# One more half chunk projected by seven block products, and three weight sums moved from the Vector engine to GpSimd

## The chip, the cores and the metric

The kernel runs on one core of a Trainium2 chip. The engines of that core have short names in the profile: PE (TensorE, matrix products; PEld is its weight load), DVE (VectorE), ACT (ScalarE), POOL (GpSimd) and SP (SyncE, whose queue issues all DMAs of this kernel). The metric is the device time of one execution in microseconds (us), the median over several runs.

## The reference

A DeltaNet layer is followed by a two-layer MLP without gating.

```python
# q, k, v: (4, 8, 768, 48); beta: (4, 8, 768)
k_n = k / (norm(k) + 1e-6)
for t in range(768):
    y[:, :, t] = q[:, :, t] @ state
    v_old = state^T k_n[:, :, t]
    state += beta[:, :, t] * outer(k_n[:, :, t], v[:, :, t] - v_old)
# y -> x of shape (3072, 384); w_in (384, 2048), w_out (2048, 384), both float64
h = x @ w_in
g = h / (1 + exp(-h))
out = g @ w_out          # (3072, 384) float32
```

## The kernel before

The sequence of 768 tokens is cut into six chunks of 128. In each chunk the four batches with eight heads each are worked on together. A chunk goes through these steps: `prepare` (transposes of keys and queries, and the score blocks of each head), `invert` (a unit triangular matrix in each 32 by 32 block is inverted), `solve` (the inverses are merged to larger blocks, the new values are found and the states updated) and `feed_forward` (the MLP on the 512 tokens of the chunk, in two halves `hf` of two batches each).

`feed_forward(c)` is a generator. Each `next` issues one piece of the MLP, and the program deals these pieces out by hand between the steps of the next chunk's attention. Within each engine the order of instructions is fixed: `pin` ties every instruction to the one issued before it on its engine, and `in_line` does the same for the DMAs of SP. So the order of the calls is the order in which each engine works, and an engine whose next instruction waits does nothing else.

A half of the MLP has two parts. `hidden(c, hf)` makes eight tiles `phid` in PSUM, each from 12 profile records on PE (a matrix product of 32-bit numbers shows as two records); ACT turns each by Silu into `gT` (L729). The tiles rotate through a pool `psM` of two PSUM buffers, so PE can be at most two tiles ahead of ACT. The second part is the product with `w_out`. There are two ways to do it:

- `project(c, b, o)`, used for both halves of chunk 0: for each of two batches, 16 products with 384 columns each, eight pieces of two products.
- `combine(c, hf)`, used in all later chunks: the two batches are the two rows of a 2 by 2 block matrix, `gT`'s even and odd feature blocks are its columns, and `w_out` is a 2 by 2 block matrix as well. Seven products of blocks (Winograd's form of Strassen's method) take the place of eight. It has seven chains of eight products with 192 columns, 14 pieces of four products each. It needs sums of blocks of `g`, made by DVE in `sum_g` (named S1 to S4), and sums of blocks of `w_out`, made once by `sum_w`.

`sum_w` has eight steps of 128x768 elements each: six write the three tiles `sums_of_w`, and the last two overwrite one block of `w_out` in place. The in-place steps destroy values that `project` still needs, so they have to stand behind the last `project`. All eight are DVE instructions (L776), the six behind `invert(1)` and the two within `prepare(2)`.

`invert(c)` is a chain of rank-one updates on DVE, 30 pairs of a product (L477) and an addition (L481), each waiting for the one before it, both with two inputs in SBUF. At its end ACT copies one half of the result (L485) and DVE the other (L486), SP writes both to DRAM and reads them back in the layout that `solve` wants (L492, L502). The generator yields 32 times.

GpSimd, before `invert(1)` starts, does the integer additions of `narrow` (L181), which makes 32-bit weights from the 64-bit ones. Its last instruction before `solve(1)` is the last of these.

The part of the program that the change touches begins after `prepare(1)`: 22 of chunk 0's 64 pieces have been issued when the loop over `invert(1)` starts, that is all of `hidden(0, 0)` and six pieces of `project`. The loop and the lines behind it deal out 28 more before `solve(1)`, which takes 12, and the last two follow it.

Of the kernel before, what the change touches and what calls it, by code (L numbers as in the profile page):

```python
# [21 lines left out]
def kernel(  # L22
# [22 lines left out]
    nc = tc.nc  # L45
# [15 lines left out]
    FG = 3  # L61
# [12 lines left out]
    def bank(pool, tag, name):  # L74
        return pool.tile([P, 512], FP32, name=name, tag=tag)
# [3 lines left out]
    def behind(later, earlier, how=NoSync):  # L79

        tc.add_manual_dep(
            later.ins, earlier.ins.name,
            mybir.DependencyInfo(how, mybir.DependencyReason.DATA), reason="order",
        )
# [3 lines left out]
    def pin(op):  # L88

        engine = op.ins.engine  # L90
        if engine in pins:
            behind(op, pins[engine])
        pins[engine] = op
        return op
# [35 lines left out]
    def load_v(i):  # L130
        if i < N and i not in vfs:
            vfs[i] = load.tile([P, H, D], FP32, name="vf", bufs=4)
            in_line(nc.sync.dma_start(out=vfs[i][:], in_=chunk_of(v, i)))
# [123 lines left out]
    for t in bkbufs:  # L257
# [4 lines left out]
        out=above[:], in_=above[:], pattern=[[1, P]], compare_op=ALU.is_gt, fill=0.0,  # L262
# [33 lines left out]
    def squares(c):  # L296

        sums[c] = small.tile([P, BH], FP32, name="ss", bufs=1)[:]
        for b in range(B):
            if c == 1:  # L300
                sq = packed(zbufs[b])
            else:
                if b % HB == 0:
                    two = work.tile([P, HB, H, D], FP32, name="sq", tag="xg"[b // HB], bufs=1)
                sq = two[:, b % HB]
            pin(nc.scalar.activation(
                out=sq, in_=packed(kbufs[(c * B + b) % NK]), func=ACTF.Square
            ))
            pin(nc.vector.tensor_reduce(
                out=sums[c][:, b * H : (b + 1) * H], in_=sq, axis=AX.X, op=ALU.add  # L310
            ))
# [401 lines left out]
    def hidden(c, hf):  # L713

        for f in range(NFF // 2):
            ph = bank(psM, "m", "phid")
            for j in range(2):
                for a in range(NKT):
                    pin(nc.tensor.matmul(  # L719
                        ph[:, j * GT : (j + 1) * GT],  # L720
                        lhsT=w_in[:, a, (2 * f + j) * P : (2 * f + j + 1) * P],
                        rhs=xTs[c, hf][:, a, :],
                        start=(a == 0), stop=(a == NKT - 1),
                    ))
                if j == 0:
                    yield
            if f % FG == 0:
                gTs[f // FG] = mlp.tile([P, FG, 2 * GT], FP32, name="gT", bufs=3)
            pin(nc.scalar.activation(  # L729
                out=gTs[f // FG][:, f % FG, :], in_=ph[:], func=ACTF.Silu, scale=0.5  # L730
            ))
            if c > 0 and f % FG == 1 and f >= FG:
                for which in (S1, S2):
                    sum_g(which, f // FG - 1)
            yield

    def project(c, b, o):

        po = bank(psM, "m", "po")
        for f in range(NFF):  # L740
            at = (f % 2) * GT + (b % HB) * C
            pin(nc.tensor.matmul(  # L742
                po[:, 0:DM], lhsT=gTs[f // 2 // FG][:, f // 2 % FG, at : at + C],
                rhs=w_outs[f // HFF][:, f % HFF, :], start=(f == 0), stop=(f == NFF - 1),
            ))
            if f == NFF - 1:
                pin(nc.scalar.mul(o[:, b % HB], po[:, 0:DM], 0.5))
                row = b * S + c * C
                in_line(nc.sync.dma_start(out=out[row : row + C, :], in_=o[:, b % HB]))
            if f % 2 == 1:  # L750
                yield
# [6 lines left out]
    def quarters(i, j, m):  # L758
        t = w_outs[i][:].rearrange("p (a j) (n m) -> p a j n m", j=2, n=2)
        return t[:, :, j, m]  # L760

    def sum_w():


        n = HFF // 2
        for k, left, right, op in (
            (0, (1, 1), (0, 1), ALU.subtract), (1, 0, (0, 0), ALU.add), (2, (1, 0), 1, ALU.subtract),
            (None, (0, 1), (0, 0), ALU.subtract),
        ):
            for i in range(2):  # L770
                of = [
                    quarters(i, *x) if isinstance(x, tuple) else sums_of_w[x][:, n * i : n * (i + 1)]
                    for x in (left, right)
                ]
                to = of[0] if k is None else sums_of_w[k][:, n * i : n * (i + 1)]
                yield pin(nc.vector.tensor_tensor(out=to, in0=of[0], in1=of[1], op=op))  # L776


    S1, S2, S3, S4 = (
# [7 lines left out]
    def sum_g(which, g):  # L787
        k, left, right, op = which
        fs = group(g)
        of = [  # L790
            sums_of_g[:, x, fs] if isinstance(x, int) else
            gTs[g][:, 0 : fs.stop - fs.start, x[0] * GT + x[1] * C : x[0] * GT + (x[1] + 1) * C]
            for x in (left, right)
        ]
        pin(nc.vector.tensor_tensor(out=sums_of_g[:, k, fs], in0=of[0], in1=of[1], op=op))  # L795
# [64 lines left out]
    def feed_forward(c):  # L860
        for hf in range(2):
            yield from hidden(c, hf)
            if c > 0:
                yield from combine(c, hf)
                continue
            o = mlp.tile([P, HB, DM], FP32, name="o", bufs=1)
            for b in range(hf * HB, (hf + 1) * HB):
                yield from project(c, b, o)
# [4 lines left out]
    def go(steps, n=1):  # L873
        for _ in range(n):
            next(steps, None)

    def prepare(c, us):

        for b in range(B):
            i = c * B + b  # L880
            if len(us) == b:
                us.append(list(turn(i, A, CC))[0])
                yield
            for _ in score(i, us[b], (A, CC)):
                pass
            block_out(i, us[b])
            block_in(i)
            scale(i)
            load_k(i + B)
            size(i)  # L890
            yield
# [81 lines left out]
    def until(piece):  # L973
        while piece is not None and piece not in narrowed:
            fill(1)
# [8 lines left out]
    for b in range(B):  # L984
        size(b)
    more(1, ("in", 1))
    pieces = feed_forward(0)
    for n, _ in enumerate(solve(0, us)):
        fill(2)
# [19 lines left out]
    inv = invert(1)  # L1009
# [1 line left out]
        until(("out", min(7, n + 2)))  # L1011
        go(pieces)
    until(("out", 7))
    for n in range(20):
        go(inv, 2)
        go(pieces)
    us = next_us
    go(inv, 99)
    sums_made = sum_w()
    for n in range(8):  # L1020
        go(pieces)
        if n < 6:
            go(sums_made)
    for n, _ in enumerate(solve(1, us)):
        go(pieces, 2 if n in (1, 2) else 1)
        if n == 5:
# [3 lines left out]
    for n in range(2 * B, 3 * B):  # L1030
        load_v(n)
    go(pieces, 999)
    pieces = feed_forward(1)

    for c in range(1, NCH):
        if c + 1 < NCH:
            us = []
            for n, _ in enumerate(prepare(c + 1, us)):
                go(pieces)
                if n in (2, 4):  # L1040
                    go(sums_made)
            go(pieces, 4)
            inv = invert(c + 1)
            n = 0
            for _ in inv:
                n += 1
                if n % 5 in (0, 1, 3, 4):
                    go(pieces)
            go(pieces, 7)
            for n, _ in enumerate(solve(c + 1, us)):  # L1050
                go(pieces, 2 if n in (1, 2) else 1)
                if n == 5 and c + 2 < NCH:
                    squares(c + 2)
                if n == 6 and c + 2 < NCH:
                    norms(c + 2)
            for n in range((c + 2) * B, (c + 3) * B):
                load_v(n)
        go(pieces, 999)
        if c + 1 < NCH:
            pieces = feed_forward(c + 1)  # L1060
# [30 lines left out]
```

## Time and profile before

| | us |
|---|---|
| median of 3 runs | 770.54 (770.52 to 770.78) |
| the profiled execution's own time | 770.21 |
| its span in the profile | 768.5 |
| PE busy | 730.4 (95% of the span) |
| PEld busy | 630.0 |
| DVE busy | 411.8 |
| ACT busy | 233.3 |
| POOL busy | 83.6 |
| PE work in 250 us to 768 us | without a gap in the 40-slice view, but for the last slice |
| PE idle between 140 and 171 us | 1.11, 1.80 and 1.64 |

Start times are counted from the start of the span. Engine columns of a view of windows give busy time and, in brackets, the number of instructions. In a timeline a row begins with its start and its duration, both in us, and what stands in square brackets at its end is how long the engine sat idle before it and what ended the wait. The ends of matrix products are modelled, so a busy PE isn't PE at its peak; that is why pitches (the distance of starts in a run of equal products) are used for sums over PE.

### The profile page before, as it was taken

The page shows a single profiled execution, that of the slowest core. Times are in us where ns is not written, and L with a number is a line of the kernel's source. Part 1 is how long each engine was busy: PE and PEld are TensorE (multiplying, and loading weights), DVE is VectorE, ACT ScalarE, POOL GpSimd, SP SyncE. Part 2 cuts the span into 40 slices and gives each one's busy share as a digit, 9 for nine tenths or more (in the row PEclk, how much of TensorE's full clock was granted, in tenths as well). Part 3 has the DMA queues.
Part 4 walks back from the last instruction along what each step waited for, and adds up shares of the span by engine and source line. Part 5 has one row for each costly group of instructions (what it writes and reads, how often), then busy time and mean ns, then how long its engine had stood idle before and what let it go on. Part 6 is the DMA issues. An engine that isn't in the chain of part 4 may idle for free.

```text
span 768.5 us, 16585 instructions
## 1 busy us (share of the span) xinstructions
PE 730.4 (95%) x6806; PEld 630.0 (82%) x6806; DVE 411.8 (54%) x1050; ACT 233.3 (30%) x512; POOL 83.6 (11%) x95
## 2 busy tenths in 40 slices
PE   7549799899999999999999999999999999999997
PEld 5336587478777999997999997999998999999987
DVE  4886678892336672445672445672445682221212
ACT  4524465311325212315212315212315212312020
POOL 4005246300003000002000002000002000000000
PEclk8859999999999999999999999999999999999999
DMA  9798847212025213034113044113043013010000
GB/s 164 116 167 162 172 146 194 52 66 42 13 54 106 42 48 70 6 77 101 33 49 69 5 77 96 38 49 70 5 77 77 15 49 70 5 30 0 21 1 21
DMA packets 155067, 50.93 MB, mean 66 GB/s; under 512 B 142544, under 2 KB 147536, under 8 KB 154992
## 3 DMA queue, kind: packets, MB, share of 16 engines
q1 hardware_dynamic: 154992, 49.87, 31.1%
q8 instruction: 54, 0.88, 0.5%
q14 instruction: 21, 0.17, 0.1%
HBM read 34.70 MB, written 14.16 MB: 64 GB/s over the span
## 4 chain that ended last, share of the span: by engine, by line
PE 88%; DVE 4%; DMA 3%; SPq 2%; issue 1%; ACT 1%; POOL 1%; ACTq 0%; DVEq 0%
PE phid L719 31%; PE px L813 14%; PE py L813 11%; PE pa L399 6%; PE pz L583 4%; PE pt L376 3%; PE po L742 3%; PE pw L276 3%; PE pyc L642 3%; PE pyc L614 2%; PE ph L567 2%; DMA z<-in_q_dram 2%; PE px L551 2%; PE py L551 2%; PE pu L625 2%; DVE x L481 1%
## 5 line engine op out<-in xcount | busy, mean ns | idle before, releaser
L719 PE MATMUL phid<-xT,w_in 128*128 128x256 f32 x1152 | 260.7, 382 | 2.2 <-ACT gT L729 1.6
L719 PEld LDWEIGHTS phid<-xT,w_in 128*128 128x128 f32 x1152 | 214.8, 190 | 37.2 <-issue 6.3
L729 ACT ACTIVATE gT<-phid 128x512 f32<-128x512 f32 x96 | 57.3, 598 | 189.6 <-PE phid L719 149.2
L415 DVE SCALAR_TENSOR_TENSOR ap<-pa,g,above 128x128 f32<-128x128 f32 x192 | 58.2, 376 | 43.7 <-ACT ap L409 43.7
L481 DVE TENSOR_TENSOR x<-x,rank 128x30 f32<-128x30 f32 (+9 forms) x180 | 59.6, 331 | 7.4 <-ACT x L470 1.1
L477 DVE TENSOR_TENSOR rank<-g,x 128x30 f32<-128x30 f32 (+9 forms) x180 | 59.4, 330 | 5.0
L795 DVE TENSOR_TENSOR sums_of_g<-gT 128x384 f32<-128x384 f32 (+1 forms) x60 | 29.2, 509 | 57.9 <-ACT gT L729 47.3
L813 PE MATMUL py<-w_out,sums_of_g 128*128 128x192 f32 x320 | 56.8, 329 | 0.0
L813 PE MATMUL px<-sums_of_w,sums_of_g 128*128 128x192 f32 x320 | 56.8, 329 | 0.0
L813 PEld LDWEIGHTS px<-sums_of_w,sums_of_g 128*128 128x128 f32 x320 | 52.2, 190 | 1.4 <-issue 1.4
L813 PEld LDWEIGHTS py<-w_out,sums_of_g 128*128 128x128 f32 x320 | 52.2, 190 | 0.4
L409 ACT ACTIVATE ap<-pa,g 128x128 f32<-128x128 f32 x144 | 41.6, 365 | 32.2 <-PE pa L399 32.2
L399 PE MATMUL pa<-kq 48*128 48x256 f32 x384 | 51.0, 401 | 0.2 <-DVE ap L415 0.2
L742 PE MATMUL po<-w_out,gT 128*128 128x384 f32 x128 | 44.7, 495 | 2.9 <-POOL w_out L181 2.9
L399 PEld LDWEIGHTS pa<-kq 48*128 48x128 f32 x384 | 36.9, 192 | 12.1 <-issue 8.1
L583 PEld LDWEIGHTS pz<-vf,xi 64*64 64x64 f32 x768 | 37.3, 138 | 8.5 <-issue 7.3
L583 PE MATMUL pz<-vf,xi 64*64 64x48 f32 x768 | 41.8, 224 | 0.4 <-ACT raw L170 0.3
L601 ACT COPY z<-pz 64x384 f32<-64x384 f32 x48 | 22.7, 474 | 60.8 <-PE pz L583 54.7
L438 POOL MEMSET x<- 128x1024 f32 x6 | 5.7, 950 | 313.5 <-PE pz L583 251.2
L574 DVE TENSOR_TENSOR vf<-vf,ph 128x384 f32<-128x384 f32 x20 | 11.1, 554 | 53.2 <-PE ph L567 53.2
L742 PEld LDWEIGHTS po<-w_out,gT 128*128 128x128 f32 x128 | 23.3, 190 | 18.4 <-POOL w_out L181 4.2
L574 DVE TENSOR_TENSOR vf<-vf,pz 64x384 f32<-64x384 f32 x24 | 13.4, 557 | 42.8 <-PE pz L591 26.0
(132 smaller groups left out, 924.1 us busy)
## 6 DMA issues: line engine op xcount, KB each, us to landing
kb<-in_k_dram SPq DMA_DIRECT2D x24, 192.0 KB, 3.1
z<-in_q_dram SPq DMA_DIRECT2D x24, 192.0 KB, 3.5
vf<-in_v_dram SPq DMA_DIRECT2D x24, 192.0 KB, 3.9
out_dram<-o SPq DMA_DIRECT2D x24, 192.0 KB, 2.0
blocks<-ap SPq DMA_DIRECT2D x96, 32.0 KB, 1.7
g<-blocks SPq DMA_DIRECT2D x24, 128.0 KB, 2.5
up<-x SPq DMA_DIRECT2D x6, 512.0 KB, 2.6
low<-g SPq DMA_DIRECT2D x6, 512.0 KB, 2.9
```

What stands on the lines that cost most here:

```text
L399: u["last"] = pin(nc.tensor.matmul(pa[e][:, pp * 2 * C : (pp + 1) * 2 * C], lhsT=kq[rows, 2 * g + pp, 0, :], rhs=kq[rows, 2 * g + pp, :, : ...
L409: copied = pin(nc.scalar.activation(out=ap[:, h, 0, :], in_=pa[e][:, at : at + C], func=ACTF.Copy, scale=bt[:, h : h + 1],))
L415: masked = pin(nc.vector.scalar_tensor_tensor(out=ap[:, h, j:2, :], in0=pa[e][:, at + j * C : at + 2 * C].rearrange("p (j t) -> p j t", j= ...
L477: pin(nc.vector.tensor_tensor(out=tv, in0=g[:, 0:m, m : m + 1].to_broadcast([P, m, n]), in1=x[:, m : m + 1, m + 1 : T].to_broadcast([P, m, ...
L481: yield pin(nc.vector.tensor_tensor(out=x[:, 0:m, m + 1 : T], in0=x[:, 0:m, m + 1 : T], in1=tv, op=ALU.add))
L551: pin(nc.tensor.matmul(pm[to, at : at + T], lhsT=left, rhs=right, start=True, stop=True))
L583: yield pin(nc.tensor.matmul(pzs[x][rows, h, :], lhsT=xis[x // HB][rows, x % HB * H + h, :], rhs=vs[x][rows, h, :], start=True, stop=True,))
L719: pin(nc.tensor.matmul(ph[:, j * GT : (j + 1) * GT], lhsT=w_in[:, a, (2 * f + j) * P : (2 * f + j + 1) * P], rhs=xTs[c, hf][:, a, :], star ...
L729: pin(nc.scalar.activation(out=gTs[f // FG][:, f % FG, :], in_=ph[:], func=ACTF.Silu, scale=0.5))
L742: pin(nc.tensor.matmul(po[:, 0:DM], lhsT=gTs[f // 2 // FG][:, f // 2 % FG, at : at + C], rhs=w_outs[f // HFF][:, f % HFF, :], start=(f == ...
L795: pin(nc.vector.tensor_tensor(out=sums_of_g[:, k, fs], in0=of[0], in1=of[1], op=op))
L813: pin(nc.tensor.matmul(to, lhsT=at, rhs=quarter(f, *b) if isinstance(b, tuple) else sums_of_w[b][:, f], start=start and f == 0, stop=f == ...
```

## The change

Four edits:

1. `feed_forward` takes `combine` for the second half of chunk 0 too, and `hidden` issues the sums S1 and S2 there too. Only the first half of chunk 0 still goes through `project`.
2. The six steps of `sum_w` that write `sums_of_w` go to GpSimd; the two in-place steps stay on DVE.
3. `sum_w` is made ahead of the loop over `invert(1)`. The six GpSimd steps are issued in the loop's first six rounds, the two in-place steps in the rounds 12 and 14, when all 16 pieces of the first half's `project` have been issued (the tenth round issues the last). They leave `prepare(2)`.
4. The loop has 22 rounds and not 20. Each takes two steps of `invert(1)`, but only one in every third round, so that the 32 steps last until round 19 and not round 15. Each round issues one piece. Behind the loop come six pieces and not eight.

```diff
@@ hidden @@
-            if c > 0 and f % FG == 1 and f >= FG:
+            if (c > 0 or hf > 0) and f % FG == 1 and f >= FG:
                 for which in (S1, S2):
                     sum_g(which, f // FG - 1)
@@ sum_w @@
                 to = of[0] if k is None else sums_of_w[k][:, n * i : n * (i + 1)]
-                yield pin(nc.vector.tensor_tensor(out=to, in0=of[0], in1=of[1], op=op))
+                engine = nc.vector if k is None else nc.gpsimd
+                yield pin(engine.tensor_tensor(out=to, in0=of[0], in1=of[1], op=op))
@@ feed_forward @@
             yield from hidden(c, hf)
-            if c > 0:
+            if c > 0 or hf > 0:
                 yield from combine(c, hf)
                 continue
@@ the program, after prepare(1) @@
     until(("out", 7))
-    for n in range(20):
-        go(inv, 2)
+    sums_made = sum_w()
+    for n in range(22):
+        if n < 6 or n in (12, 14):
+            go(sums_made)
+        go(inv, 2 if n % 3 else 1)
         go(pieces)
     us = next_us
     go(inv, 99)
-    sums_made = sum_w()
-    for n in range(8):
-        go(pieces)
-        if n < 6:
-            go(sums_made)
+    go(pieces, 6)
     for n, _ in enumerate(solve(1, us)):
@@ the program, prepare(2) @@
                 go(pieces)
-                if n in (2, 4):
-                    go(sums_made)
```

In the order of instructions that results, PE has seven chains of `combine` where it had 32 products of `project`, at the same places between the steps of `solve(1)`. ACT has four evictions L729 of the second half ahead of L485 and four behind it, where it had two and six. GpSimd has six instructions more, right behind its last L181. DVE has the two in-place sums within the chain of `invert(1)`, behind its 19th and its 22nd rank-one update, and the sums S1 to S4 and three additions to `o` around and within `solve(1)`. SP writes the output of the half in two DMAs together at the end.

## The prediction

> **What bounds the kernel now.** I read the busy table first: PE is busy for 730.4 of 768.5 us, so time is won or lost in PE's work or in its gaps. The chain of work that ended last, in order of time, shows which. Columns: start, duration, what.
>
> ```profile
> 168.07 0.20 DVE rank L477
> 168.30 0.20 DVE x L481
> 168.58 1.09 ACT g L485
> 169.67 0.51 ACT gT L729
> 170.22 10.63 PE phid L719 x48
> 180.85 2.58 PE po L742 x8
> ...
> 259.76 5.20 PE px L813 x32
> 264.96 2.60 PE py L813 x16
> ```
>
> From 170.22 on the chain stays on PE nearly to the end. Before that, up to 168.5, it runs along the DVE chain of `invert(1)`: PE had work, but ACT had to do L485, which waits for DVE's last update, ahead of an eviction. The timeline around it shows the gap, 1.64 us:
>
> ```profile
> 146.34 11.88 PE L742 MATMUL po<-w_out,gT 128*128 128x384 f32 x36 [1.80 <-POOL w_out L181]
> 158.05 10.52 PE L719 MATMUL phid<-xT,w_in 128*128 128x256 f32 x48
> ...
> 170.22 5.02 PE L719 MATMUL phid<-xT,w_in 128*128 128x256 f32 x22 [1.64 <-ACT gT L729]
> ```
>
> GpSimd ends its last L181 at 146.29, when DVE's chain has just begun. So the six moved sums will run beside that chain. How the two engines go together is in the timelines of DVE and of GpSimd from 122.4 to 128.5 and from 232.9 to 236.2:
>
> ```profile
> 123.73 1.44 DVE L177 SCALAR_TENSOR_TENSOR w_out<-sums_of_w,w_out 128x768 uint32<-128x768 uint32 x1
> 125.53 1.78 DVE L167 TENSOR_SCALAR w_out<-w_out 128x768 f32<-128x768 f32 x1 [0.35 <-ACT w_out L165]
> 127.34 1.07 DVE L173 TENSOR_SCALAR w_out<-w_out 128x768 uint32<-128x768 uint32 x1
> ...
> 122.51 4.37 POOL L181 TENSOR_TENSOR w_out<-w_out,raw_out 128x768 int32<-128x768 int32 x2
> 126.84 1.15 POOL L352 TENSOR_TENSOR bkb<-kb,g 128x384 f32<-128x384 f32 x1
> 127.95 1.14 POOL L360 TENSOR_TENSOR vf<-vf,n 128x384 f32<-128x384 f32 x1
> ...
> 233.91 1.52 DVE L776 TENSOR_TENSOR w_out<-w_out 128x768 f32<-128x768 f32 x1
> ...
> 234.57 1.54 POOL L360 TENSOR_TENSOR vf<-vf,n 128x384 f32<-128x384 f32 x1
> ```
>
> Undisturbed, L177 takes 0.96, L173 0.56, L776 0.95, L352 and L360 0.83. Each is longer here by what it waits for the other. They take turns: L167 ends at 127.30 (125.53 + 1.78), L173 is ready 0.03 later, but GpSimd, waiting since 126.84, goes first and ends at 127.99; L173 ends at 128.41, 0.42 behind it; L360 then ends 0.69 behind that.
>
> **What the Trainium skill says.** "SBUF — State Buffer", section "Who interferes with whom": a DVE instruction with two SBUF inputs contends with a GpSimd instruction that reads SBUF; who comes first has the shared port for its whole instruction, the other blocks. The rows above agree (L776 has two SBUF inputs and lost 0.57). The 60 updates of `invert` have two SBUF inputs each; none runs beside GpSimd in this trace. "GPSIMD Engine Reference", section "Performance versus the Vector engine": an fp32 tensor_tensor of 2048 elements takes 4497 ns, so an estimate for 768 is 1.69 us; the trace has 0.83 for 384 (twice that is 1.66) and 1.83 for 768 integers. "TensorE: Matmul & The Clock Gate", section "What's actually happening": after an idle window of about 3.4 us the clock is halved, and a busy window restores it. The trace agrees: PEclk 0.50 after the wait up to 48.92, full again at about 54.6.
>
> **Part by part.** Counts of matrix products are records, two each.
>
> *Seven products.* Removed: 64 records with 384 columns, pitch 2.58/8 = 0.3225 us, 20.6 us. Added: 112 with 192 columns, pitch 2.60/16 = 0.1625, 18.2 us. PE gains **2.4 us**. The breaks between pieces are as many, and cost the same 0.2 us. S1 to S4 are 8 DVE operations of 0.55 and 4 of 0.42, 6.1 us, and three additions to `o` of 0.35, 0.56 and 0.35; DVE has 1.1 to 1.7 of each 5 us busy in `solve(1)` from 185 to 205, and the same sums ride along in `solve(2)`, where PE shows no gap (20.00 of 20.00 busy from 300 to 320). I cost them at nothing; should a `vf` addition fall behind a 1.5 us block of S3 or S4, PE waits at most about 1 us. The two output DMAs stand behind `solve`'s DMAs in SP's queue, busy to 228.6 anyway, ahead of loads of `v` not needed for 60 us: nothing.
>
> *Pieces moved into the loop.* L485 now stands behind four evictions of `phid`, not two. PE can so make six tiles before it stalls, not four: 72 records at 10.63/48 = 0.2215 from 158.05 on, to **173.9**. The seventh waits for the fifth's eviction, which stands behind L485. From L485's start to PE's is 170.22 - 168.58 = 1.64. So the chain may be later by 173.9 - 170.22 = **3.7 us** before PE stalls; with no delay the old gap of 1.64 is gone.
>
> *Two in-place sums inside the chain.* 0.95 plus 0.03 of issue each: **2.0 us** later. Their PE wait (`project`'s last product, 158.2) and GpSimd wait are over when DVE gets there, after 161.
>
> *Six sums on GpSimd.* 1.7 us each (bounds 1.57, twice the 0.785 between starts of L352 and L360, and 1.83). Below nothing is excluded: the DVE sums they replace stood behind the chain, so nothing in the chain gets shorter. GpSimd waits for nothing but its own results, so the six compete with the first updates. Taking turns, each holds DVE up for its length less the 0.14 that each side overlaps (0.56 - 0.42, 0.83 - 0.69) and the 0.03 of issue: 1.7 - 0.31 = 1.4. Six, and the start: **8.5 us** (7.6 to 9.3). Behind the sums in GpSimd's queue stand the memsets L438 and L439, due at 207. If the port weren't contended it would be 0. I take 8.5, as three rows with two SBUF inputs (L177 at 123.73 and at 130.66, L776) all were blocked. The sums are done by about 157, long before chain 2 of `combine` reads the third.
>
> *Sum.* The chain ends 10.5 us late. PE resumes at 170.22 + 10.5 = 180.7 and has idled 180.7 - 173.9 = 6.8 us where it idled 1.64: **+5.2**. An idle stretch of 6.8 us holds a whole clock window, so PE resumes at half speed. After 48.92 it stayed there 5.7 us, after 11.91 about 5.2, after 85.36 3.4; half of that is lost. Depending on the window's phase I take 2.1 (1.3 to 3.0): **+2.1**. What is late next is L492's and L502's DMAs: `xi` was asked for until 178.65 and took 2.6, so would land at 181.3 + 10.5 = 191.8; `solve(1)`'s first merges come at about 195 (188.29 + 5.2 + 2.1), and those that read `xi` later: no new wait. Behind them PE is back to back.
>
> +5.2 + 2.1 - 2.4 = **+4.9 us**. On the profiled execution's 770.21 (span 768.5) that is 775.1; this execution lies 0.33 below the median, so on the median 770.54 + 4.9 = **775.4**.
>
> **Rivals.**
>
> 1. *The chain isn't held up* (faster): GpSimd and the updates go side by side, or DVE's next update, 0.03 us behind the last, always gets the port first and the sums wait for the chain's end. For it: no update is seen beside GpSimd; starved sums would still be ready near 181, ahead of chain 2 at about 185. Against: L173 was as close behind L167 and lost the port. The chain is then 2.0 late, under the 3.7: no stall, 770.5 - 1.64 - 2.4 = **766.5**. It decides below a delay of 3.7 us, that is, if at most one of the six sums collides; with a delay of 7.7 us (5.7 with the clock's loss) gain and loss cancel.
> 2. *The stall without the clock's loss*: the window's phase leaves the clock up. Against: 6.8 us is two windows. 775.4 - 2.1 = **773.3**.
> 3. *DVE is late inside `solve(1)` as well*: S3 and S4 ahead of `vf` additions, or dearer GpSimd sums (over 1.83). For it: where S4 stands before the second batch's addition, PE has a piece (1.49) and a step's products (1.06) to do while DVE does an addition (0.56) and S4 (1.5), so about 0.5 us is to spare. 775.4 + 2.5 = **778**.
>
> **How the numbers follow.** Main case 0.70, rival 1 0.10, rival 2 (and partial contention, 770 to 773) 0.10, rival 3 0.10. The main case's own range is 773.6 (7.6 + 2.0 of delay, 1.3 of clock: +3.1) to 777.1 (9.3 + 2.0, 3.0: +6.6). Over all cases the range is 772.8 to 778.0, which leaves out rival 1 and about a third of the others. A change of 0.2% (1.5 us) is about what a measurement can tell from none. Faster by more: rival 1, 0.10. Within: a part of rival 2's partial contention, 0.03. Slower: 0.87.
>
> **What would show it.** DVE: the first six updates alternate with L777 on GpSimd (L776 of before), each held up by about 1.4 us; L481's last end moves from 168.5 to about 179. PE: 72 `phid` records without a gap from 158, then idle to about 181 (released by gT L729, behind L485), PEclk 0.5 for some us after it, and 112 L814 records in place of 64 of `po`. I am wrong if the updates keep their pace while L777 runs, or if PE has no gap over 4 us between 170 and 185.

## The result and the profile after

The changed kernel takes 775.66 us (median of 9 runs, 773.84 to 778.30) where the kernel before takes 771.75 (9 runs beside it, 770.52 to 773.83). The ratio is 1.0053, with a 95% interval of 1.0036 to 1.0071: slower by about half a percent. The profiled execution took 775.38 us, its span is 773.7.

The runs of one kernel lie several us apart. In the traces the spread is in the stretch ahead of `invert(1)`, which no kernel of this study changes: the first rank-one update of `invert(1)` starts at 146.44 us before, at 146.75 in the changed kernel, and between 142.45 and 150.18 in the experiments. From that update to the end of the span the time repeats far better. I call this stretch the tail. It is 768.503 - 146.436 = 622.07 us before and 773.674 - 146.748 = 626.93 after, so the change costs **4.86 us** there. The medians differ by 775.66 - 771.75 = 3.91 us, and the ratio's interval is 2.8 to 5.5 us.

How well the tail repeats is seen behind the last `phid` record of chunk 0's second half, from where on PE does the same work in all changed versions: to the end of the span it is 585.21 to 585.23 us in nine of the ten traces of changed versions, 585.34 in the one with the sums on GpSimd behind the chain, and 587.66 before. So behind that record every changed version gains 2.3 to 2.4 us, and all that is lost is lost ahead of it. Line numbers of the changed kernel from `sum_w` on are higher by one, so L776 is L777 now, L813 is L814.

The chain that ended last, in order of time (start, duration, what):

```profile
178.93 0.20 DVE rank L477
179.16 0.20 DVE x L481
...
179.43 1.08 ACT g L485
180.52 0.51 ACT gT L729
...
181.07 7.39 PE phid L719 x24
188.46 2.60 PE px L814 x16
```

It has the same order as before, but DVE's last update stands at 179.16 and not at 168.30, and 24 records of `phid` take 7.39 us, where 48 took 10.63. The timeline of PE:

```profile
146.66 11.88 PE L742 MATMUL po<-w_out,gT 128*128 128x384 f32 x36 [1.82 <-POOL w_out L181]
158.37 15.70 PE L719 MATMUL phid<-xT,w_in 128*128 128x256 f32 x72
181.07 7.39 PE L719 MATMUL phid<-xT,w_in 128*128 128x256 f32 x24 [6.99 <-ACT gT L729]
```

PE makes six tiles in one run (72 records), then stands still for 6.99 us until ACT has done L485 and the next eviction. It is the only gap on PE from here to the end of the kernel, as the 1.64 us was before. What held DVE up is seen in the timelines of DVE and of GpSimd:

```profile
146.75 1.80 DVE L477 TENSOR_TENSOR rank<-g,x 128x30 f32<-128x30 f32 x1
148.65 1.68 DVE L481 TENSOR_TENSOR x<-x,rank 128x30 f32<-128x30 f32 x1
150.37 1.74 DVE L477 TENSOR_TENSOR rank<-g,x 128x58 f32<-128x58 f32 x1
152.14 1.73 DVE L481 TENSOR_TENSOR x<-x,rank 128x58 f32<-128x58 f32 x1
153.91 1.75 DVE L477 TENSOR_TENSOR rank<-g,x 128x84 f32<-128x84 f32 x1
155.70 1.74 DVE L481 TENSOR_TENSOR x<-x,rank 128x84 f32<-128x84 f32 x1
157.47 0.27 DVE L477 TENSOR_TENSOR rank<-g,x 128x108 f32<-128x108 f32 x1
```

```profile
146.68 3.58 POOL L777 TENSOR_TENSOR sums_of_w<-w_out 128x768 f32<-128x768 f32 x2
150.23 3.56 POOL L777 TENSOR_TENSOR sums_of_w<-sums_of_w,w_out 128x768 f32<-128x768 f32 x2
153.76 3.57 POOL L777 TENSOR_TENSOR sums_of_w<-w_out,sums_of_w 128x768 f32<-128x768 f32 x2
```

Six updates that need 0.19 to 0.25 us each take 1.7 to 1.8, one for each of the six sums. With the last sum the waits end: the next update takes 0.27. Before, the same updates ran like this:

```profile
146.44 0.19 DVE L477 TENSOR_TENSOR rank<-g,x 128x30 f32<-128x30 f32 x1
146.81 0.21 DVE L481 TENSOR_TENSOR x<-x,rank 128x30 f32<-128x30 f32 x1 [0.18 <-ACT x L470]
147.05 0.22 DVE L477 TENSOR_TENSOR rank<-g,x 128x58 f32<-128x58 f32 x1
```

The lost time lies within the updates' own records and not in idle time ahead of them, where a wait for another engine's signal would show, as the 0.18 us for ACT does here. GpSimd's sums aren't slowed: they start 1.77 us apart and take 1.80, and one that starts while DVE stands idle (the third in the version with the sums on GpSimd behind the chain) takes 1.81. So the engines take turns, one update to each sum, but beside these short updates DVE alone pays for it. The view of windows shows what the gap did to PE's clock (columns: stretch, its length, then PE, PEld, DVE, ACT and POOL busy, PEclk, DMA share, GB/s):

```profile
174.00:178.00 4.00, 0.08 (x1) 0.00 (x0) 3.66 (x12) 0.00 (x0) 0.00 (x0) 1.00 0.00 0
178.00:181.00 3.00, 0.00 (x0) 0.00 (x0) 2.76 (x9) 1.57 (x3) 0.00 (x0) 0.53 0.27 111
181.00:185.00 4.00, 3.93 (x9) 3.20 (x10) 1.15 (x3) 0.50 (x2) 0.00 (x0) 0.50 0.57 198
185.00:188.00 3.00, 3.00 (x15) 2.60 (x14) 0.00 (x0) 0.60 (x1) 0.00 (x0) 0.99 0.79 125
```

PEclk falls to 0.50 within the gap and stays there until 185, four us into the work behind it.

### The profile page after: what moved, and what is told of

Read it like the earlier page. It is cut to its first block, busy times and chain, and to the rows that moved or that the text cites. A ratio compares the mean times of both kernels' runs of the same rounds, so it can differ in the third digit from the quotient of the medians.

```text
span 773.7 us, 16695 instructions
## 1 busy us (share of the span) xinstructions
PE 729.9 (94%) x6854; PEld 637.8 (82%) x6854; DVE 420.4 (54%) x1059; ACT 233.2 (30%) x513; POOL 93.7 (12%) x101
## 4 chain that ended last, share of the span: by engine, by line
PE 86%; DVE 5%; DMA 4%; SPq 2%; issue 1%; ACT 1%; POOL 1%; ACTq 0%; DVEq 0%
PE phid L719 30%; PE px L814 15%; PE py L814 12%; PE pa L399 5%; PE pz L583 4%; PE pt L376 3%; PE pw L276 3%; PE pyc L642 3%; PE pyc L614 2%; PE ph L567 2%; DVE rank L477 2%; DMA z<-in_q_dram 2%; DVE x L481 2%; PE px L551 2%; PE py L551 2%; PE pu L625 2%
## 5 line engine op out<-in xcount | busy, mean ns | idle before, releaser
L729 ACT ACTIVATE gT<-phid 128x512 f32<-128x512 f32 x96 | 57.3, 598 | 191.5 <-PE phid L719 171.3
L415 DVE SCALAR_TENSOR_TENSOR ap<-pa,g,above 128x128 f32<-128x128 f32 x192 | 58.2, 376 | 46.2 <-ACT ap L409 46.2
L481 DVE TENSOR_TENSOR x<-x,rank 128x30 f32<-128x30 f32 (+9 forms) x180 | 64.2, 356 | 7.3 <-ACT x L470 0.9
L796 DVE TENSOR_TENSOR sums_of_g<-gT 128x384 f32<-128x384 f32 (+1 forms) x66 | 32.2, 510 | 64.8 <-ACT gT L729 54.1
L477 DVE TENSOR_TENSOR rank<-g,x 128x30 f32<-128x30 f32 (+9 forms) x180 | 64.1, 356 | 5.0
L814 PE MATMUL py<-w_out,sums_of_g 128*128 128x192 f32 x352 | 62.9, 329 | 0.0
L814 PE MATMUL px<-sums_of_w,sums_of_g 128*128 128x192 f32 x352 | 62.9, 329 | 0.0
L814 PEld LDWEIGHTS px<-sums_of_w,sums_of_g 128*128 128x128 f32 x352 | 57.4, 190 | 1.8 <-issue 1.7
L814 PEld LDWEIGHTS py<-w_out,sums_of_g 128*128 128x128 f32 x352 | 57.4, 190 | 0.8 <-issue 0.3
L276 PE MATMUL pw<-state,ident 128*128 128x384 f32 x80 | 30.9, 532 | 4.0 <-DVE state L140 2.8
L814 PE MATMUL py<-w_out,gT 128*128 128x192 f32 x176 | 32.3, 332 | 0.0
```

Source lines behind the costliest of these rows:

```text
L276: done = pin(nc.tensor.matmul(pw[:, 0:DM], lhsT=ident[:], rhs=states[B - 1][:].rearrange("p a w -> p (a w)")[:, 0:DM], start=True, stop=Tr ...
L415: masked = pin(nc.vector.scalar_tensor_tensor(out=ap[:, h, j:2, :], in0=pa[e][:, at + j * C : at + 2 * C].rearrange("p (j t) -> p j t", j= ...
L477: pin(nc.vector.tensor_tensor(out=tv, in0=g[:, 0:m, m : m + 1].to_broadcast([P, m, n]), in1=x[:, m : m + 1, m + 1 : T].to_broadcast([P, m, ...
L481: yield pin(nc.vector.tensor_tensor(out=x[:, 0:m, m + 1 : T], in0=x[:, 0:m, m + 1 : T], in1=tv, op=ALU.add))
L729: pin(nc.scalar.activation(out=gTs[f // FG][:, f % FG, :], in_=ph[:], func=ACTF.Silu, scale=0.5))
L814: pin(nc.tensor.matmul(to, lhsT=at, rhs=quarter(f, *b) if isinstance(b, tuple) else sums_of_w[b][:, f], start=start and f == 0, stop=f == ...
```

## The experiments

All edits are made to the changed kernel. Tails come from one profiled execution each. A ratio is to runs of the kernel before beside it on the same chip; not all rows come from one chip, so ratios can be compared and medians can't. The ratios' intervals are 0.2% to 0.5% to each side (1.3 to 3.5 us), so differences of one or two us between versions are read from the tails alone. "Chain" is the time from the start of the first to the end of the last rank-one update of `invert(1)`.

| kernel | chain | PE gap | tail | median | ratio to before (95%) |
|---|---|---|---|---|---|
| before | 22.05 | 1.64 | 622.07 | | |
| changed | 32.60 | 6.99 | 626.93 | 775.66 | 1.0053 (1.0036 to 1.0071) |
| sums on DVE behind the chain | 22.06 | none | 617.72 | 765.83 | 0.9925 (0.9899 to 0.9952) |
| sums on GpSimd behind the chain | 22.06 | none | 617.85 | 766.47 | 0.9937 (0.9912 to 0.9962) |
| seven products alone | 22.05 | 1.61 | 619.61 | 768.39 | 0.9945 (0.9924 to 0.9966) |
| PE kept busy in the gap | 32.56 | 0.52 | 624.98 | 772.87 | 1.0016 (0.9996 to 1.0037) |
| two sums on GpSimd | 25.08 | none | 617.72 | 768.75 | 0.9969 (0.9941 to 0.9997) |
| four sums on GpSimd | 28.10 | 2.49 | 622.16 | 771.37 | 1.0012 (0.9993 to 1.0031) |
| six sums, in-place sums behind | 31.09 | 5.47 | 625.06 | 776.00 | 1.0055 (1.0034 to 1.0077) |
| memsets on GpSimd | 23.17 | none | 617.72 | 766.78 | 0.9953 (0.9923 to 0.9983) |
| loop of before | 32.55 | 12.11 | 632.73 | 780.85 | 1.0159 (1.0113 to 1.0205) |

### All weight sums on the Vector engine, behind the chain

```diff
-                engine = nc.vector if k is None else nc.gpsimd
+                engine = nc.vector
@@
-    sums_made = sum_w()
     for n in range(22):
-        if n < 6 or n in (12, 14):
-            go(sums_made)
         go(inv, 2 if n % 3 else 1)
         go(pieces)
     us = next_us
     go(inv, 99)
+    go(sum_w(), 8)
     go(pieces, 6)
```

> The changed kernel with all eight weight sums back on the Vector engine, together behind the chain of invert(1); seven products and the loop of 22 rounds stay. Contention theory: the chain loses its 9.0 us of waits and 1.5 us of in-place sums, ends near 168.5, PE makes all eight phid tiles without a gap: 1.64 (the old gap) + 2.4 (seven products) less than before, 766.5 us on a before of 770.5, ratio about 0.995. Rival, that the extra rounds or the seven products themselves hold PE up: the gap of 7.0 us stays in part and the time stays above before.

PE's timeline has the eight tiles in one run:

```profile
161.80 20.88 PE L719 MATMUL phid<-xT,w_in 128*128 128x256 f32 x96
182.52 2.76 PE L814 MATMUL px<-w_out,gT 128*128 128x192 f32 x16
```

The tail is 617.72, 4.35 us shorter than before and 9.21 shorter than the changed kernel's. So the seven products and the extra pieces in the loop are a gain, and the whole loss lies in where the sums stand. This version beats both kernels: ratio to before 0.9925 (0.9899 to 0.9952).

### The sums on GpSimd, but behind the chain

```diff
-    def sum_w():
+    def sum_w(first=None):
@@
-                yield pin(engine.tensor_tensor(out=to, in0=of[0], in1=of[1], op=op))
+                done = pin(engine.tensor_tensor(out=to, in0=of[0], in1=of[1], op=op))
+                if first is not None:
+                    behind(done, first, Sync)
+                    first = None
+                yield done
@@
-    sums_made = sum_w()
+    chain_end = None
     for n in range(22):
-        if n < 6 or n in (12, 14):
-            go(sums_made)
-        go(inv, 2 if n % 3 else 1)
+        for _ in range(2 if n % 3 else 1):
+            chain_end = next(inv, None) or chain_end
         go(pieces)
     us = next_us
-    go(inv, 99)
+    sums_made = sum_w(chain_end)
+    go(sums_made, 6)
     go(pieces, 6)
+    go(sums_made, 2)
```

> The six sums stay on GpSimd, but the first waits for the last instruction of the chain of invert(1), and the two in-place sums stand behind it too. Contention theory: what costs is the overlap in time and not the engine, so the chain ends near 168.5 and PE has no gap before the keys; sums of 1.8 us each are ready near 181, or 184 where they collide with the sums of g, against chain 2 of the products at about 185: 766.5 to 768 us. Rival, that sums on GpSimd are simply too slow for what reads them: PE waits in chain 2, a gap of several us there and a time near or above before.

The timeline of GpSimd shows the same six sums, now from 168.99 on:

```profile
168.99 4.07 POOL L777 TENSOR_TENSOR sums_of_w<-w_out 128x768 f32<-128x768 f32 x2 [23.00 <-DVE g L486]
173.03 3.89 POOL L777 TENSOR_TENSOR sums_of_w<-sums_of_w,w_out 128x768 f32<-128x768 f32 x2
176.88 3.89 POOL L777 TENSOR_TENSOR sums_of_w<-w_out,sums_of_w 128x768 f32<-128x768 f32 x2
```

The first wait, 23.00 us, is the one that this version makes. The sums are ready at 176.88 + 3.89 = 180.77, and chain 2 of the products, the first that reads one of them, starts at 184.74; PE has no gap:

```profile
184.74 1.49 PE L818 MATMUL px<-sums_of_w,gT 128*128 128x192 f32 x8
```

The tail is 617.85, within 0.13 of the version with the sums on DVE. GpSimd isn't the wrong engine for them here. What costs is that they run beside the chain.

### Seven products alone

```diff
-                engine = nc.vector if k is None else nc.gpsimd
+                engine = nc.vector
@@
-    sums_made = sum_w()
-    for n in range(22):
-        if n < 6 or n in (12, 14):
-            go(sums_made)
-        go(inv, 2 if n % 3 else 1)
+    for n in range(20):
+        go(inv, 2)
         go(pieces)
     us = next_us
     go(inv, 99)
-    go(pieces, 6)
+    go(sum_w(), 8)
+    go(pieces, 8)
```

> Only the seven products in chunk 0's second half: loop of 20 rounds as before, all eight weight sums on the Vector engine behind the chain. If seven products are worth 2.4 us and nothing else changes, the gap of 1.64 us ahead of the fifth phid tile stays, and the time is 768.1 us on a before of 770.5, ratio 0.997. Rival, that the sums of g, which it adds to the Vector engine around solve(1), take the gain back: ratio 1.000 and gaps on PE between 185 and 225.

```profile
154.07 10.52 PE L719 MATMUL phid<-xT,w_in 128*128 128x256 f32 x48
166.21 10.63 PE L719 MATMUL phid<-xT,w_in 128*128 128x256 f32 x48 [1.61 <-ACT gT L729]
```

PE's timeline is that of before, with its gap. The tail falls by 622.07 - 619.61 = 2.46 us. So the seven products give what the pitches say (2.4), and the sums of `g` that they need cost PE next to nothing. The step from here to the version with all sums behind the chain, 619.61 - 617.72 = 1.89, is the worth of the pieces moved into the loop: the 1.61 us gap and 0.28 more. Nearly all of the rest lies in the `phid` records: two runs of 48 take 10.52 + 10.63 = 21.15, one run of 96 takes 20.88.

### PE kept busy in the gap

```diff
         go(inv, 2 if n % 3 else 1)
         go(pieces)
+    for _ in range(10):
+        busy()
     us = next_us
```

> The changed kernel with ten idle products (2 records of 384 columns each, 6.5 us in all, result unused) on PE where it stood still for 7.0 us. Nothing else moves. If the halved clock after the gap costs 2.1 us, the 24 phid records behind the gap take 5.3 us and not 7.4, and the time falls by 2.1 us against the changed kernel, to ratio about 1.0035 over before where the changed kernel has 1.006. Rival, that these records were slow because they waited for evictions one by one: no change.

```profile
172.28 6.61 PE L276 MATMUL pw<-state,ident 128*128 128x384 f32 x20
179.42 5.45 PE L719 MATMUL phid<-xT,w_in 128*128 128x256 f32 x24 [0.52 <-ACT gT L729]
```

The idle products fill the gap but for 0.52 us. The 24 records behind it take 5.45 us and not 7.39, and the tail falls by 626.93 - 624.98 = 1.95 us. So about two of the 4.9 us were lost after the gap, to the halved clock, and not to evictions that came one by one. The ratio of the medians, 1.0016, is lower than the 1.0035 that I expected, which still lies within its interval.

### Two, four and six sums on GpSimd beside the chain

In all three the in-place sums stand behind the chain. The diff is that of four sums; the others have `k in (0,)` and 2, or `k in (0, 1, 2)` and 6.

```diff
-                engine = nc.vector if k is None else nc.gpsimd
+                engine = nc.gpsimd if k in (0, 1) else nc.vector
@@
     sums_made = sum_w()
     for n in range(22):
-        if n < 6 or n in (12, 14):
+        if n < 4:
             go(sums_made)
         go(inv, 2 if n % 3 else 1)
         go(pieces)
     us = next_us
     go(inv, 99)
+    go(sums_made, 8)
     go(pieces, 6)
```

> Two of the six sums on GpSimd beside the chain of invert(1), the other four and the two in-place sums on the Vector engine behind it; the rest as in the changed kernel. I count from the first rank-one update of invert(1) to the end of the span, since the stretch ahead of it differs by some us from execution to execution: 622.1 us before, 626.9 in the changed kernel, 617.7 with all sums on the Vector engine behind the chain. Contention theory: the chain is 2 x 1.5 = 3.0 us late, under the 3.7 that PE can bridge: no gap, 617.7. Rival, that the first collision alone upsets the chain or that any delay reaches PE: a gap of 1 us or more.

> Four of the six sums on GpSimd beside the chain, the rest on the Vector engine behind it. Contention theory: the chain is 4 x 1.5 = 6.0 us late, 2.3 over what PE can bridge: a gap of 2.3 us, no loss of clock, since that is less than a window, and from the first update to the end 617.7 + 2.3 = 620.0 us. Rival, that the delay grows otherwise than by one wait for each sum: a chain later by something clearly other than 6.

> All six sums on GpSimd beside the chain as in the changed kernel, but the two in-place sums behind the chain. Contention theory: the chain is 9.0 us late and not 10.5, the gap on PE 5.4 and not 7.0. From the first update to the end 617.7 + 5.4 = 623.1 us, and up to 3 more if a whole clock window falls into the gap. Rival, that the in-place sums cost nothing: gap of 7.0 as in the changed kernel.

The chain grows from 22.05 to 25.08, 28.10 and 31.09 us: 3.03, 6.05 and 9.04 more, 1.51 for each sum. The gap on PE is none, 2.49 and 5.47. Delay less gap is 3.56 with four, 3.57 with six, and 10.55 - 6.99 = 3.56 in the changed kernel, so that is the delay that PE can bridge. Two sums stay below it, and the tail is 617.72, to the hundredth that of no sums on GpSimd. In-place sums inside the chain cost it 10.55 - 9.04 = 1.51 us, and the tail 626.93 - 625.06 = 1.87. With six sums the tail of 625.06 lies within the 3 us that I gave the clock above 623.1.

With four sums I was wrong on the clock. I had expected none of it lost in a gap that short; the tail is 2.2 us over my number. PE's timeline, and its windows behind the gap:

```profile
175.55 7.13 PE L719 MATMUL phid<-xT,w_in 128*128 128x256 f32 x24 [2.49 <-ACT gT L729]
```

```profile
175.00:176.00 1.00, 0.45 (x2) 0.43 (x3) 1.00 (x2) 0.98 (x2) 0.00 (x0) 1.00 1.03 414
176.00:177.00 1.00, 1.00 (x7) 0.83 (x6) 1.00 (x2) 0.00 (x0) 0.00 (x0) 0.95 1.02 410
177.00:178.00 1.00, 1.00 (x4) 0.82 (x3) 1.00 (x2) 0.00 (x0) 0.00 (x0) 0.50 0.24 90
```

The 24 records take 7.13 us, though the gap was only 2.49: the clock is halved at about 176.9, more than 1 us after PE had started again. With six sums they take 7.04 behind a gap of 5.47.

The clock's own records in the traces show what the loss follows. Halved stretches last 3.41 us with four and with six sums (from 176.90 in both) and 6.83 in the changed kernel (178.21 to 185.04); all others in these eleven traces, but for one cut off at the end of each kernel, are whole multiples of 3.41 too (up to 23.89). So the clock changes on a grid of 3.41 us, and what is lost is half of the part of a halved stretch in which PE works: 3.41, 3.25 and 3.97 us with four sums, with six and in the changed kernel, hence 1.7, 1.6 and 2.0 us, where the records took 1.8, 1.7 and 2.1 us longer. So the length of the gap doesn't set the loss: 5.47 us cost less than 2.49. The grid interval ahead of the drop with four sums, 173.48 to 176.90, holds 2.06 us of the gap; before, the whole gap of 1.64 us lies in one interval (167.29 to 170.71) and no drop follows. Where between the two the limit is, if it is idle time that decides, isn't shown.

### GpSimd writes, but doesn't read, beside the chain

```diff
-                engine = nc.vector if k is None else nc.gpsimd
+                engine = nc.vector
@@
-    sums_made = sum_w()
+    for _ in range(6):
+        pin(nc.gpsimd.memset(sums_of_w[0][:], 0.0))
     for n in range(22):
-        if n < 6 or n in (12, 14):
-            go(sums_made)
         go(inv, 2 if n % 3 else 1)
         go(pieces)
     us = next_us
     go(inv, 99)
+    go(sum_w(), 8)
     go(pieces, 6)
```

> All sums on the Vector engine behind the chain, but GpSimd writes zeros six times to a tile of 128x1536 (1.37 us each, overwritten later) beside the first updates of the chain: it only writes SBUF and reads nothing. If the engines compete for reading the second input, the updates keep their pace, and from the first update to the end it is 617.7 us. If any GpSimd instruction holds the Vector engine up, the chain is about 6 x 1.1 = 6.4 us late, PE has a gap of 2.7, and it is 620.4 us.

GpSimd's six memsets run back to back from 148.31, 8.56 us in all. In the timelines of GpSimd and of DVE:

```profile
148.31 8.56 POOL L1016 MEMSET sums_of_w<- 128x1536 f32 x6
...
147.50 2.24 DVE L468 COPY x<-g 128x16 f32<-128x16 f32 x3 [1.21 <-DMA g<-blocks]
148.40 1.35 DVE L477 TENSOR_TENSOR rank<-g,x 128x30 f32<-128x30 f32 x1
149.87 0.21 DVE L481 TENSOR_TENSOR x<-x,rank 128x30 f32<-128x30 f32 x1
150.12 0.22 DVE L477 TENSOR_TENSOR rank<-g,x 128x58 f32<-128x58 f32 x1
```

All updates but the first keep their pace beside the memsets. The first is late by 1.1 us together with the copy L468 ahead of it, which ends at 149.74, about when the first memset does (148.31 + 1.38). The tail is 617.72. So a rank-one update doesn't compete with just any work of GpSimd: it waits for sums, which read SBUF, and not for memsets, which only write it. The Trainium skill has it so ("SBUF — State Buffer", section "Who interferes with whom": a two-input instruction doesn't contend with one that only writes). For the copy L468, with one input, the same section names another case, the two-port modes that copies can enter, which contend with GpSimd; the wait of L468 fits it, but no run here shows in which mode L468 works.

### The loop of before

```diff
-    for n in range(22):
+    for n in range(20):
         if n < 6 or n in (12, 14):
             go(sums_made)
-        go(inv, 2 if n % 3 else 1)
+        go(inv, 2)
         go(pieces)
     us = next_us
     go(inv, 99)
-    go(pieces, 6)
+    go(pieces, 8)
```

> The changed kernel with the loop of before: 20 rounds of two steps of invert(1), eight pieces behind it. All sums stay where the change puts them. Theory: the copy on ACT at the chain's end now stands behind two evictions and not four, so PE stops after four phid tiles, 10.6 us behind its start, and not after six, 15.7. The chain ends as late as in the changed kernel, so the gap is 7.0 + 5.2 = 12.2 us, and from the first update to the end it is 626.9 + 5.2 = 632.1 us, up to 1 more or less by the clock. Rival, that the extra pieces don't matter since ACT or PE are late for another reason: 626.9.

```profile
158.32 10.52 PE L719 MATMUL phid<-xT,w_in 128*128 128x256 f32 x48
180.96 13.26 PE L719 MATMUL phid<-xT,w_in 128*128 128x256 f32 x48 [12.11 <-ACT gT L729]
```

PE stops after four tiles instead of six, and the gap grows by 5.12. The tail is 632.73, 5.80 more than the changed kernel's. Of the 0.7 beyond the gap the clock took about 0.55: the 48 records take 13.26 us where they took 10.63 before, 2.63 more, against 2.08 in the changed kernel. So the fourth edit took 5.8 us off the damage of the second and third, and gives 1.9 where there is none.

## Why the prediction was right

It said 775.4 us, from +5.2 of gap, +2.1 of clock and -2.4 of products. Measured: 775.66 us, and a tail longer by 4.86 us where the sum said 4.9. The mechanism and each step came as foretold, but that the figures agree so closely is in part luck. The 775.4 was built on a median of 770.54 from three runs; the nine runs beside the changed kernel have 771.75, and the medians differ by 3.91 and not 4.9. And two terms were off by half a us each, in opposite directions. Step by step:

- **Seven products, -2.4.** -2.46 in the version with them alone.
- **What PE can bridge, 3.7.** 3.56 in each of three kernels with a gap. I had let the six tiles end at 173.9; on that scale they end at 174.07 - 0.31 = 173.76.
- **Six sums, +8.5.** 9.04. The term was too small: a sum takes 1.80 us and not 1.7, so each costs the chain 1.51 and not 1.4. It lies within the bounds of 7.6 to 9.3.
- **Two in-place sums, +2.0.** 1.51. The term was too large: each starts while the update ahead is still finishing (170.31, where that ends at 170.40), and the next update starts while the sum finishes (171.18, where that ends at 171.26). The two misses nearly cancel: 10.55 where I had 10.5.

```profile
170.00 0.40 DVE L481 TENSOR_TENSOR x<-x,rank 128x228 f32<-128x228 f32 x1
170.31 0.95 DVE L777 TENSOR_TENSOR w_out<-w_out 128x768 f32<-128x768 f32 x1
171.18 0.38 DVE L477 TENSOR_TENSOR rank<-g,x 128x220 f32<-128x220 f32 x1
```

- **The clock, +2.1.** 24 records took 7.39 us; at the pitch of 0.2215 they take 5.31. That is 2.08; keeping PE busy gave 1.95 of it back. The range was 1.3 to 3.0, so that the middle of it was met so closely is luck.
- **Gain and loss cancel at a delay of 5.7** (rival 1). With four sums the chain is 6.05 late, and the tail of 622.16 is that of before, 622.07.
- **No new wait on the DMAs of `up` and `low`, and none in `solve(1)`** (rival 3). PE has no gap behind 181.07 in the changed kernel.
- **Rival 1, the chain isn't held up.** Refuted for sums beside the chain. My reason against it was only in part the right one: the row from which I read who goes first, L173, has one input in SBUF and the updates have two. That updates with two inputs, 0.03 us behind one another, lose their turn in the same way was first shown by the changed kernel. The gain of 4.0 us that rival 1 counts with is about that of the two versions with the sums behind the chain: their tails are 4.35 and 4.22 shorter than before.
- **Rival 2, no loss of clock.** Refuted by PEclk 0.50 from 178.2 to 185 and by the version with PE kept busy. My reason for the loss, that the gap holds a whole window, was stricter than need be: a gap of 2.49 us was enough.

That the Vector engine waits for GpSimd's sums is shown by the trace, one long update to each sum, and by the dose of two, four and six. That it is the reading of a second input from SBUF is shown from two sides. Write-only memsets on GpSimd leave the updates alone. And the trace of before has a DVE instruction, L415, with one tensor in PSUM (`pa`) and one in SBUF (`above`), besides one number for each partition:

```profile
121.39 2.42 DVE L415 SCALAR_TENSOR_TENSOR ap<-pa,g,above 128x128 f32<-128x128 f32 x8
230.97 2.43 DVE L415 SCALAR_TENSOR_TENSOR ap<-pa,g,above 128x128 f32<-128x128 f32 x8 [2.76 <-ACT ap L409]
```

The first eight ran beside GpSimd's additions, which were at work from 121.73 on, the second eight while GpSimd stood idle (until 232.99), and they took the same time. What a GpSimd instruction with a single input does to the updates wasn't tried.

## What to carry to other kernels

Work moved to an idle GpSimd isn't free for DVE: look at what DVE does at that time. Beside a chain of small DVE instructions with two SBUF inputs each GpSimd sum cost the chain most of its own length (1.51 of 1.80 us). Six of them turned a gain of 4.35 us into a loss of 2.99, and with the two in-place sums in the chain into one of 4.86; the same six sums on GpSimd behind the chain cost 0.13. When PE is fed from the end of such a chain, work out first how much delay its buffers bridge (here 3.6 us), and reckon with a halved clock behind a gap that opens: here it cost about 2 us behind gaps of 2.49 us and more.

## What was not expected of the hardware

- A PE gap of 2.49 us was followed by a halved clock, which came more than 1 us after PE had resumed, and cost 7.13 - 5.31 = 1.8 us. A gap of 5.47 cost 1.7, one of 6.99 cost 2.1: half of what PE did in the halved stretches, which come in multiples of 3.41 us. The gap of 1.64 us in the kernel before was followed by none.
- An fp32 sum of 768 elements on GpSimd takes 1.80 us, more than twice the 0.83 of 384 elements, and just as long beside the updates as when it starts with DVE idle (1.81). Beside the short updates only DVE lost time; beside the sums of `g`, of 0.55 us, GpSimd's sums took up to 2.13.
- An in-place sum put between two updates of the chain added less than it lasts: 0.95 us long, 0.75 us of delay, since it overlapped the updates on both sides.
